# Channels-first inputs, kG transposed on TensorE and one weight row per FFN step in a gated linear attention with a gated FFN

## The chip, the cores and the metric

The kernel runs on one core of a Trainium2 chip. The metric is device time in microseconds (us). The engines are TensorE (PE; its weight loads are PEld), VectorE (DVE), ScalarE (ACT), GpSimd (POOL) and SyncE (SP), which here only issues transfers.

## The reference

For batch 4, 8 heads, 768 positions and 48 channels per head, a state of 48 x 48 per head is decayed by channel and added to, position by position; the outputs are the tokens of a gated feed-forward net (FFN).

```
state = alpha[t][:, None] * state + outer(k[t], v[t])
y[t]  = q[t] @ state
x     = y, heads side by side                   # 3072 x 384
gate  = 1 / (1 + exp(-(x @ w_gate)))            # w_gate, w_val 384 x 1536
out   = (gate * (x @ w_val)) @ w_out            # w_out 1536 x 384
```

q, k, v and alpha come as float32, the three weights as float64.

## The kernel before

**Attention.** The work is cut into 32 units, each of 384 tokens and two heads; four units (a group) fill the 384 x 384 tile of tokens that one FFN group needs, and there are eight groups. A unit treats its tokens in six chunks of 64, so that the recurrence becomes products. Its two heads lie on partitions 0 to 47 and 64 to 111, channels on partitions and tokens along the row.

- alpha, k and q are loaded with tokens on partitions (L343) and turned to `az`, `kT`, `qT` by VectorE (`turn`, L377).
- `G` (L386) is a scan of alpha backwards, the product of alpha to the end of a chunk; `F` (L398) a scan of its inverse; `dec` (L393) the decay over a chunk; `kt = kT * G` (L397); `xa`, `xb` = `qT * F`, one half per head (L411).
- The products of a unit on TensorE are the scores `kt^T x` (L425), masked to the lower triangle by VectorE (L460) or GpSimd (L455); what each chunk adds to the state (L470), for which `kn`, the turned `kt`, is the stationary operand; and the outputs (L511). `kn` comes for units 0 to 9 from TensorE transposes (L420) and four ScalarE copies (L438), and from unit 10 on (`TV`) from eight VectorE transposes (L443).
- The six states before the chunks are VectorE's (`st`, L489), their decayed copies GpSimd's or VectorE's (L502). The output is split into an exact pair of parts of twelve bits, `yt` (L529, L535), and written by transfers into the group's token tile `x` (L542).

**FFN.** A group has 12 steps; a step is 128 hidden channels of 384 tokens. `pg` and `pv` (L184) are nine products of 128 x 384 each: three tiles of input channels times three pairings of the parts. ScalarE makes `sg = sigmoid(pg)` (L580), VectorE `hf = pv * sg` (L581), ScalarE its high part `hh` (L583), GpSimd its low part `hl` (L586). The nine return products into three banks `po` (L596, with h as the stationary operand) of step n stand on TensorE behind `pg` and `pv` of step n + 1. At a group's end `po` goes through `ob` (L610) to the output.

**Weights.** A third of a step's weights (gate, value or out) is one transfer of 384 KB into one of four raw buffers (L304). Turning float64 into two parts takes per third: a scaling (ScalarE, L306), a shift (ScalarE L310 or VectorE L313), an and (VectorE L315), a shift-or (VectorE L317), the high part (ScalarE, L320) and the low part (GpSimd or VectorE, L322). All this is done once, during group 0; later groups find the weights in SBUF.

**Order.** Every part of the program is given to `Plan` with an engine, an estimated time and a key that says when it is wanted; the planner lays the parts out with these and writes each engine's instruction list. Tables by unit (`UNITS`, `SHIFTS`, `LOWS`) say which engine has a piece. The first two groups of units run as fast as they can, mixed with the weights; from group 1 on a unit is put between `pv` and `po` of every third step. 45 small products (`warm`, L563) come ahead of step 0.

## Time and profile before

| | us |
|---|---|
| device time, median of 3 runs (lowest, highest) | 625.47 (624.29, 626.53) |
| the profiled execution's span, first to last instruction | 622.7 |
| TensorE busy | 571.5 (92%) |
| VectorE busy | 444.6 (71%) |
| ScalarE busy | 214.9 (35%) |
| GpSimd busy | 264.5 (42%) |

The profiled execution's span is 2.8 us under the median of the device times: what lies before the first and behind the last instruction shown is not in the span. Busy shares over the span mix three stages: up to 45 us step 0 has not begun; up to 154 us the weights arrive and steps 0 to 11 run; from 179 us on TensorE has work all the time.

### The profile page before, as it was taken

How to read it: one execution, taken by the hardware profiler on the slowest of the kernel's cores; microseconds unless marked ns; L12 is line 12 of the kernel's file. 1: busy time of each engine (PE TensorE's matmuls, PEld its weight loads, DVE VectorE, ACT ScalarE, POOL GpSimd, SP SyncE). 2: the span in 40 equal slices, each digit the busy share in tenths (PEclk: the TensorE clock that was granted, in tenths of full speed). 3: DMA queues.
4: the chain of work that ended last, by engine and by line, in shares of the span. 5: the costliest groups of instructions: out<-in, count | busy, mean ns of one | idle time of the engine just before them, and what ended most of it. 6: DMA issues, size and time to landing. Idle time of an engine off the chain costs nothing.

```text
span 622.7 us, 13152 instructions
## 1 busy us (share of the span) xinstructions
PE 571.5 (92%) x5069; PEld 534.1 (86%) x5069; DVE 444.6 (71%) x1013; ACT 214.9 (35%) x515; POOL 264.5 (42%) x301
## 2 busy tenths in 40 slices
PE   6786867688889999999999999999999999999995
PEld 3566756567779999999899999999999999999994
DVE  8998999999987777888677777777777755211111
ACT  2558677575222222222222232222222221222121
POOL 5546597663433333434344444333344433212210
PEclk8968997999999999999999999999999999999998
DMA  9977954874345161423416161505141111001001
GB/s 193 231 201 185 235 148 139 196 225 105 103 99 132 26 155 47 114 54 88 119 31 138 31 176 28 133 20 155 41 104 30 46 51 30 20 20 39 1 0 44
DMA packets 58759, 61.20 MB, mean 98 GB/s; under 512 B 29440, under 2 KB 41728, under 8 KB 58688
## 3 DMA queue, kind: packets, MB, share of 16 engines
q1 hardware_dynamic: 58496, 59.99, 39.0%
q8 instruction: 41, 0.67, 0.5%
q0 software_dynamic: 192, 0.30, 0.2%
q14 instruction: 30, 0.25, 0.1%
HBM read 46.10 MB, written 4.72 MB: 82 GB/s over the span
## 4 chain that ended last, share of the span: by engine, by line
PE 55%; DVE 23%; DMA 10%; issue 5%; ACT 3%; SPq 3%; POOL 0%; DVEq 0%; ACTq 0%
PE pv L184 17%; PE po L596 17%; PE pg L184 16%; DVE kn L443 3%; DVE st L489 3%; DVE wraw L315 3%; DMA out_dram<-ob 2%; DVE wraw L317 2%; PE at L511 2%; PE at L425 2%; SPq L343 2%; PE at L470 2%; DMA raw_a<-in_alpha_dram 1%; DVE hf L581 1%; DVE az L377 1%
## 5 line engine op out<-in xcount | busy, mean ns | idle before, releaser
L586 POOL TENSOR_TENSOR hl<-hf,hh 128x384 fp32r<-128x384 f32 x95 | 99.6, 1048 | 239.1 <-ACT hh L583 237.6
L581 DVE TENSOR_TENSOR hf<-pv,sg 128x384 f32<-128x384 f32 x96 | 53.2, 554 | 133.9 <-PE pv L184 133.0
L184 PE MATMUL pg<-x,wgh 128*128 128x384 f32 x576 | 118.3, 340 | 10.2 <-ACT wgh L320 6.4
L184 PE MATMUL pv<-x,wvh 128*128 128x384 f32 x576 | 118.7, 341 | 8.9 <-DVE hf L581 6.3
L184 PEld LDWEIGHTS pg<-x,wgh 128*128 128x128 f32 x576 | 101.5, 189 | 12.9 <-ACT wgh L320 7.6
L184 PEld LDWEIGHTS pv<-x,wvh 128*128 128x128 f32 x576 | 101.7, 190 | 12.6 <-DVE hf L581 8.9
L583 ACT CAST hh<-hf 128x384 fp32r<-128x384 f32 x96 | 49.4, 514 | 180.5 <-DVE hf L581 180.3
L596 PE MATMUL po<-woh,hh 128*128 128x384 f32 x288 | 100.9, 350 | 2.2 <-ACT hh L583 2.2
L596 PE MATMUL po<-woh,hl 128*128 128x384 f32 x288 | 98.2, 342 | 1.2 <-POOL hl L586 1.1
L596 PE MATMUL po<-wol,hh 128*128 128x384 f32 x288 | 97.7, 339 | 0.0
L580 ACT ACTIVATE sg<-pg 128x384 f32<-128x384 f32 x96 | 46.9, 489 | 135.7 <-PE pg L184 135.6
L184 PE MATMUL pv<-x,wvl 128*128 128x384 f32 x288 | 67.0, 339 | 2.2 <-POOL wvl L322 2.0
L184 PE MATMUL pg<-x,wgl 128*128 128x384 f32 x288 | 67.1, 340 | 0.8 <-DVE wgl L322 0.7
L443 DVE STREAM_TRANSPOSE kn<-kt 32x192 f32<-32x192 f32 x176 | 65.1, 370 | 2.4
L596 PEld LDWEIGHTS po<-woh,hh 128*128 128x128 f32 x288 | 54.7, 190 | 4.7 <-ACT hh L583 2.7
L411 POOL TENSOR_TENSOR xb<-qT,F 64x384 f32<-64x384 f32 x28 | 36.7, 1312 | 49.5 <-PE at L511 47.0
L596 PEld LDWEIGHTS po<-woh,hl 128*128 128x128 f32 x288 | 54.6, 190 | 2.5 <-POOL hl L586 2.3
L184 PEld LDWEIGHTS pv<-x,wvl 128*128 128x128 f32 x288 | 51.4, 189 | 4.1 <-POOL wvl L322 2.9
L596 PEld LDWEIGHTS po<-wol,hh 128*128 128x128 f32 x288 | 54.7, 190 | 0.0
L184 PEld LDWEIGHTS pg<-x,wgl 128*128 128x128 f32 x288 | 51.8, 190 | 2.1 <-DVE wgl L322 1.0
L489 DVE SCALAR_TENSOR_TENSOR st<-st,dec,at 128x48 f32<-128x48 f32 x180 | 46.5, 258 | 4.4
L386 DVE TENSOR_TENSOR_SCAN G<-az,d1g 128x384 f32<-128x384 f32 x32 | 33.6, 1052 | 0.2
(172 smaller groups left out, 906.0 us busy)
## 6 DMA issues: line engine op xcount, KB each, us to landing
x<-yt SPq DMA_DIRECT2D x48, 144.0 KB, 3.0
wraw<-in_moe_w_val_dram SPq DMA_DIRECT2D x12, 384.0 KB, 4.5
wraw<-in_moe_w_gate_dram SPq DMA_DIRECT2D x12, 384.0 KB, 4.2
wraw<-in_moe_w_out_dram SPq DMA_DIRECT2D x12, 384.0 KB, 4.1
out_dram<-ob SPq DMA_DIRECT2D x21, 192.0 KB, 2.1
raw_a<-in_alpha_dram SPq DMA_DIRECT2D x28, 140.0 KB, 3.8
raw_k<-in_k_dram SPq DMA_DIRECT2D x28, 140.0 KB, 2.9
raw_q<-in_q_dram SPq DMA_DIRECT2D x28, 140.0 KB, 3.4
```

Source lines behind the costliest of these rows:

```text
L184: nc.tensor.matmul(out=dst, lhsT=lhs(a, i), rhs=rhs(b, i), start=(n == 0 and i == 0), stop=(n == len(todo) - 1 and i == NK - 1))
L315: plan.add("vector", 0.27, key, lambda: nc.vector.tensor_scalar(out=half[:, :, :, 0, 1], in0=half[:, :, :, 1, 1], scalar1=0x8000, scalar2= ...
L317: plan.add("vector", 0.47, key, lambda: nc.vector.scalar_tensor_tensor(out=lower, in0=upper, scalar=3, in1=lower, op0=ALU.logical_shift_le ...
L386: plan.add("vector", 0.47, t[0], lambda: nc.vector.tensor_tensor_scan(out=G[:, ::-1], data0=az[:, N:0:-1], data1=d1g, initial=0.0, op0=ALU ...
L411: plan.add(e, 0.96 if e == "gpsimd" else 0.47, t[2], lambda x=x, lo=lo, hi=hi, e=e: getattr(nc, e).tensor_tensor(out=x[lo:hi], in0=qT[lo:h ...
L443: plan.add("vector", 0.27, t[10], lambda fr=fr, to=to, par=par, late=late: nc.vector.transpose(out=kn[to:to + 32, :, 32 * late:32 * late + ...
L489: nc.vector.scalar_tensor_tensor(out=st[:, c + 1, :], in0=st[:, c, :], scalar=dec[:, c:c + 1], in1=pd[:, c * D:(c + 1) * D], op0=ALU.mult, ...
L580: plan.add("scalar", 0.38, key + 1.5, lambda: nc.scalar.activation(out=sg, in_=got["g"][1][:, 0:N], func=AF.Sigmoid), [got["g"][0]], [sgn])
L581: plan.add("vector", 0.47, key + 2.9, lambda: nc.vector.tensor_tensor(out=hf, in0=got["v"][1][:, 0:N], in1=sg, op=ALU.mult), [got["v"][0], ...
L583: plan.add("scalar", 0.41, key + 2.9, lambda: nc.scalar.copy(out=hh, in_=hf), [hfn], [hhn])
L586: plan.add(e, 0.47 if last else 0.96, key + 2.9, lambda: getattr(nc, e).tensor_tensor(out=hl, in0=hf, in1=hh, op=ALU.subtract), [hfn, hhn] ...
L596: nc.tensor.matmul(out=pt[:, 0:DM], lhsT=h[a][:, t * P:(t + 1) * P], rhs=weights.part("o", b, f), start=(f == 0 and i == 0), stop=(f == NF ...
```

## The change

The computation is the same, with the same units, steps and pairs of parts. What moves:

- **Inputs.** The host lays alpha, k and q out channels first (`laid_out`, layout only): per head pair and unit one row for each of 128 partitions with a0 (alpha at the chunks' starts), az (alpha with zeros there), k and q, 1159 numbers, 593 KB, with the unused partitions included; v likewise in chunks. The VectorE turns L377, the copy of a0 and the memsets of az are gone. k times G is written in place (L380 after), by GpSimd for every unit.
- **kG.** It is transposed on TensorE (L403 after, three products with the identity) and copied by ScalarE for every unit; the VectorE transposes L443 are gone.
- **Weights.** One transfer per step of 1.18 MB (`weights_in[f]`, L309 after), converted in two halves of 576 columns (step 0: three of 384). The shift is always ScalarE's (L322 after), the low part always GpSimd's (L330 after); VectorE has the and (L324) and the shift-or (L326). Two raw buffers in place of four of a third of the size: steps 0, 2, 4, 6, 8, 10 and 11 use the first, the others the second, whose place is later that of step 11's weights.
- **FFN step.** `hf` overwrites `sg`, of which there is one buffer. In the return, w_out is stationary and h moves, and the products with `hh` of all three banks stand ahead of those with `hl`. The output leaves transposed (the host turns it back), through three buffers that lie in the first raw buffer.
- **Engines and order.** Masks are always VectorE's, the decayed states always GpSimd's, q times F one half each (L394). All loads are issued by SP; before, GpSimd issued v of the first two units. A unit's products are spread over three steps. There are 60 `warm` products in place of 45.

```diff
-        plan.add("vector", 0.47, t[0], lambda: turn(az[:, 0:N], 0), loaded[u, 0], [an])
...
+        plan.add("sync", (0.475, P * (hi - lo) * 4 / 250e3), t["load"], lambda lo=lo, hi=hi: nc.sync.dma_start(
+            out=tin[:, lo:hi], in_=rows[b, p, :, base + lo:base + hi]), writes=[(inn, m) for m in marks])
...
+        a0, az, kT, qT = tin[:, a_0:a_z], tin[:, a_z:a_k], tin[:, a_k:a_q], tin[:, a_q:col]
...
-        turned = u >= TV
-        if not turned:
-            plan.add("tensor", (0.325, 0.9), t[9], transposes, [ktn], [pkn])
...
-                        out=kn[to:to + 32, :, 32 * late:32 * late + 32],
-                        in_=kt[fr:fr + 32].rearrange("p (c s) -> p c s", c=NC)[:, :, 32 * par:32 * par + 32]),
...
+        plan.add("tensor", (0.109 * nb, 0.9), t["X"], transposes, [(inn, "k")], [pkn])
...
+        rn, raw = raws[f % 2 if f < NF - 1 else 0]
+        plan.add("sync", (0.475, 4.9), key - 1.0, lambda: nc.sync.dma_start(out=raw.rearrange("p a b -> p (a b)"), in_=weights_in[f]),
+                 writes=[((rn, i), m) for i in range(3) for m in "ul"])
+        cuts = (0, DM, 2 * DM, WF) if f == 0 else (0, WF // 2, WF)
...
+            plan.add("gpsimd", pool_(n), kk, lambda lower=lower, lo=lo, hi=hi: nc.gpsimd.tensor_tensor(
+                out=weights.tile(f)[:, 1, lo:hi], in0=lower.bitcast(F32), in1=weights.tile(f)[:, 0, lo:hi], op=ALU.subtract),
...
-        plan.add("vector", 0.47, key + 2.9, lambda: nc.vector.tensor_tensor(
-            out=hf, in0=got["v"][1][:, 0:N], in1=sg, op=ALU.mult), [got["v"][0], sgn], [hfn])
...
+        plan.add("vector", vec(T), s - 100, lambda: nc.vector.tensor_tensor(
+            out=sg, in0=got["v"][1][:, 0:T], in1=sg, op=ALU.mult), [got["v"][0]], [sgn])
...
+                nc.tensor.matmul(out=pso_now[m][1][:, 0:T], lhsT=weights.part("o", b, f)[:, m * P:(m + 1) * P], rhs=h[a][:, 0:T],
+                                 start=(f == 0 and i == 0), stop=(f == NF - 1 and i == 2))
```

VectorE in the steady part, one unit and what stands around it (`st` is a state, `pv` times `sg` the gated product). Before:

```order
L460 TENSOR_TENSOR xa_130<-at_154,mask 64x384
L460 TENSOR_TENSOR xb_132<-at_154,mask 64x384
L443 STREAM_TRANSPOSE kn_133<-kt_127 32x6x32 x8
L377 STREAM_TRANSPOSE kT_124<-raw_k_78 128x12x32
L581 TENSOR_TENSOR hf_147<-pv_158,sg_146 128x384
L398 SCALAR_TENSOR_TENSOR F_122<-az_80,d1f_82 128x384
L377 STREAM_TRANSPOSE qT_125<-raw_q_79 128x12x32
L386 SCALAR_TENSOR_TENSOR G_121<-az_81,d1g 128x384
L377 STREAM_TRANSPOSE az_80<-raw_a_77 128x12x32
L389 TENSOR_SCALAR G_115<-G_121 128x6
L393 TENSOR_TENSOR dec_119<-a_113,G_121 128x6
```

After, the same pieces of a unit:

```order
L542 TENSOR_TENSOR sg_111<-pv_120,sg_111 128x384
L371 SCALAR_TENSOR_TENSOR G_92<-in_78,d1g 128x384
L373 TENSOR_SCALAR G_96<-G_92 128x6
L378 TENSOR_TENSOR dec_98<-in_78,G_92 128x6
L375 RECIPROCAL d1f<-G_96 128x6
L376 SCALAR_TENSOR_TENSOR F_94<-in_78,d1f 128x384
L542 TENSOR_TENSOR sg_111<-pv_120,sg_111 128x384 x2
L394 TENSOR_TENSOR xa_88<-in_78,F_94 64x384
L457 SCALAR_TENSOR_TENSOR st_109<-st_109,dec_101,at_117 128x48 x6
L506 TENSOR_TENSOR yt_86<-at_118,yt_86 128x384
L440 TENSOR_TENSOR xa_89<-at_118,mask 64x384
```

The eight transposes to `kn` and the three turns are gone; the scans read the loaded tile `in`, and the unit's other pieces stand between the same FFN products as one list.

SP while the weights come, the transfers of the weights (`wraw` before, `raw` and `first_w` after) and what stands between them (`x` is the token tile, `va` and `vb` hold v). Before:

```order
L304 DMA wraw_143<-in_moe_w_gate_dram 128x3x256
L542 DMA x_145<-yt_135 48x768 x2
L304 DMA wraw_141<-in_moe_w_out_dram 128x768
L343 DMA raw_a_77<-in_alpha_dram 32x2x560 x2
L343 DMA raw_k_78<-in_k_dram 32x2x560
L304 DMA wraw_144<-in_moe_w_val_dram 128x3x256
L343 DMA raw_k_78<-in_k_dram 32x2x560 x3
L373 DMA va_86<-in_v_dram 64x6x48
L373 DMA vb_88<-in_v_dram 64x6x48
L304 DMA wraw_142<-in_moe_w_gate_dram 128x3x256
```

After:

```order
L514 DMA x_756<-yt_86 48x768
L359 DMA in_79<-in_rows_dram 128x1159
L514 DMA x_756<-yt_86 48x768
L309 DMA raw_84<-in_w_dram 128x2304
L364 DMA va_81<-in_vc_dram 64x288
L364 DMA vb_83<-in_vc_dram 64x288
L514 DMA x_756<-yt_87 32x768
L309 DMA first_w_76<-in_w_dram 128x2304
L514 DMA x_756<-yt_87 16x768
L359 DMA in_78<-in_rows_dram 128x1159
L364 DMA va_80<-in_vc_dram 64x288
L514 DMA x_756<-yt_87 48x768
```

A row of weights for `raw` or `first_w` now waits for the conversion of the row before it in that place, and loads of units and writes of tokens stand behind it.

TensorE in the steady part, a step with a unit. Before:

```order
L596 MATMUL po_161<-woh_64,hl_153 128x384
L184 MATMUL pg_157<-x_933,wgh_1228 128x384 x6
L184 MATMUL pg_157<-x_933,wgl_1242 128x384 x3
L184 MATMUL pv_158<-x_933,wvh_1265 128x384 x6
L184 MATMUL pv_158<-x_933,wvl_1271 128x384 x3
L511 MATMUL at_156<-xa_129,va_85 48x64
L511 MATMUL at_156<-xb_131,vb_87 48x64 x2
L511 MATMUL at_156<-xa_129,va_85 48x64 x2
L511 MATMUL at_156<-xb_131,vb_87 48x64 x2
L511 MATMUL at_156<-xa_129,va_85 48x64 x2
L511 MATMUL at_156<-xb_131,vb_87 48x64 x2
```

After, a step with the transposes of one unit (the outputs, adds and scores stand in other steps):

```order
L555 MATMUL po_122<-hl_115,w_804 128x384
L555 MATMUL po_123<-hl_115,w_804 128x384
L213 MATMUL pg_119<-x_110,w_1024 128x384 x9
L403 MATMUL at_118<-ident,in_79 128x128 x3
L213 MATMUL pv_120<-x_110,w_1024 128x384 x9
L555 MATMUL po_121<-hh_112,w_949 128x384 x2
L555 MATMUL po_122<-hh_112,w_949 128x384 x2
L555 MATMUL po_123<-hh_112,w_949 128x384 x2
L555 MATMUL po_121<-hl_114,w_949 128x384
L555 MATMUL po_122<-hl_114,w_949 128x384
L555 MATMUL po_123<-hl_114,w_949 128x384
```

Before, the small products of a unit stand together between `pv` and `po`; after, the three transposes stand alone between `pg` and `pv`, and the return has its `hh` products first.

## Rows read from the trace of the kernel before

**Rows 1.** This is the busy time of each engine in four stretches. Columns: stretch, its length, then for each engine the busy us and the instructions, PEclk (the granted clock of TensorE as a share of full speed), the busy share of the DMA engines, GB/s. The edges are the starts of `pg` of step 0 (45.48), step 12 (153.79) and step 16 (178.72) and the end of the last product (615.29).

```profile
0.00:45.48 45.48, 34.59 (x471) 22.15 (x472) 41.91 (x104) 20.89 (x57) 25.24 (x45) 0.81 0.93 209
45.48:153.79 108.31, 83.18 (x713) 71.48 (x712) 105.31 (x197) 75.79 (x163) 69.44 (x63) 0.94 0.67 178
...
178.72:615.29 436.57, 433.30 (x3779) 422.15 (x3779) 273.15 (x662) 110.57 (x275) 161.04 (x183) 1.00 0.27 66
615.29:622.70 7.41, 0.01 (x1) 0.00 (x0) 0.43 (x1) 0.48 (x1) 0.00 (x0) 0.74 0.27 91
```

**Rows 2.** This is the fourth part of the page, the chain that ended last, by engine.

```profile
PE 55%; DVE 23%; DMA 10%; issue 5%; ACT 3%; SPq 3%; POOL 0%; DVEq 0%; ACTq 0%
```

**Rows 3.** This is the chain that ended last, one FFN step with a unit and the start of the next (start, us, what).

```profile
398.69 1.56 PE pv L184 x9
400.26 0.81 PE at L511 x24
401.06 0.67 PE at L470 x24
401.74 0.71 PE at L425 x24
402.45 1.77 PE po L596 x9
404.22 1.56 PE pg L184 x9
```

**Rows 4.** This is the same chain at the end: the last step's 18 return products.

```profile
612.14 3.17 PE po L596 x18
```

**Rows 5.** This is TensorE's instructions in order of time, an early unit: its three transposes of `kt`, then the scores.

```profile
14.83 0.55 PE L420 MATMUL po<-ident,kt 128*128 128x128 f32 x3
15.31 0.92 PE L425 MATMUL at<-xa,kt 48*64 48x64 f32 x24
```

**Rows 6.** This is VectorE's instructions in order of time, about one unit and two FFN steps of the steady part (start, us, line, operation, out<-in). A start-to-start distance is what one costs in the row of instructions.

```profile
402.38 1.76 DVE L489 SCALAR_TENSOR_TENSOR st<-st,dec,at 128x48 f32<-128x48 f32 x6
404.15 0.56 DVE L460 TENSOR_TENSOR xa<-at,mask 64x384 f32<-64x384 f32 x1
...
405.29 3.05 DVE L443 STREAM_TRANSPOSE kn<-kt 32x192 f32<-32x192 f32 x8
408.37 0.88 DVE L377 STREAM_TRANSPOSE kT<-raw_k 128x384 f32<-128x384 f32 x1
409.10 0.54 DVE L581 TENSOR_TENSOR hf<-pv,sg 128x384 f32<-128x384 f32 x1
409.57 0.93 DVE L398 TENSOR_TENSOR_SCAN F<-az,d1f 128x384 f32<-128x384 f32 x1
410.42 0.85 DVE L377 STREAM_TRANSPOSE qT<-raw_q 128x384 f32<-128x384 f32 x1
411.13 1.04 DVE L386 TENSOR_TENSOR_SCAN G<-az,d1g 128x384 f32<-128x384 f32 x1
412.08 0.85 DVE L377 STREAM_TRANSPOSE az<-raw_a 128x384 f32<-128x384 f32 x1
412.79 0.15 DVE L389 TENSOR_SCALAR G<-G 128x6 f32<-128x6 f32 x1
...
413.28 0.56 DVE L581 TENSOR_TENSOR hf<-pv,sg 128x384 f32<-128x384 f32 x1
```

**Rows 7.** This is the same view in the first part: two of the state updates of the first units, one after the other with others between.

```profile
35.81 0.28 DVE L489 SCALAR_TENSOR_TENSOR st<-st,dec,at 128x48 f32<-128x48 f32 x1
35.99 0.28 DVE L489 SCALAR_TENSOR_TENSOR st<-st,dec,po 128x48 f32<-128x48 f32 x1
```

**Rows 8.** This is groups of VectorE's and ScalarE's instructions in the stretch of steps 0 to 11 (count, busy us, mean ns), then the two VectorE lines by themselves with their minimum, median and maximum in ns.

```profile
L315 DVE TENSOR_SCALAR wraw<-wraw 128x384 uint16<-128x384 uint16 x32 | 25.7, 803 | 1.0 <-ACT wraw L310 0.7
L317 DVE SCALAR_TENSOR_TENSOR wraw<-wraw 128x384 uint32<-128x384 uint32 x31 | 22.3, 722 | 0.0
...
L310 ACT ACTIVATE wraw<-wraw 128x384 uint16<-128x384 uint16 x19 | 20.3, 1070 | 0.0
L306 ACT ACTIVATE wraw<-wraw 128x384 f32<-128x384 f32 x32 | 18.4, 575 | 1.5 <-DMA wraw<-in_moe_w_val_dram 1.5
...
L315 DVE TENSOR_SCALAR wraw<-wraw x32: 560/626/1430, 48.0 to 153.3; 128x384 uint16<-128x384 uint16 x32
...
L317 DVE SCALAR_TENSOR_TENSOR wraw<-wraw x31: 528/570/1359, 48.9 to 149.4; 128x384 uint32<-128x384 uint32 x31
```

**Rows 9.** This is GpSimd's instructions in order of time: one in the stretch of steps 0 to 11, one in the steady part.

```profile
86.23 3.41 POOL L322 TENSOR_TENSOR wol<-wraw,woh 128x384 fp32r<-128x384 f32 x1 [0.19 <-ACT woh L320]
...
397.99 1.01 POOL L586 TENSOR_TENSOR hl<-hf,hh 128x384 fp32r<-128x384 f32 x1 [3.12 <-ACT hh L583]
```

**Rows 10.** This is the sixth part of the page, one of its transfers (count, KB each, us from issue to landing), the stretch from 20 to 40 us, and the transfer on the chain ahead of step 0.

```profile
wraw<-in_moe_w_gate_dram SPq DMA_DIRECT2D x12, 384.0 KB, 4.2
...
20.00:40.00 20.00, 14.99 (x233) 10.27 (x229) 19.51 (x48) 11.30 (x29) 12.92 (x16) 0.71 0.99 231
...
42.48 2.65 DMA x<-yt
```

**Rows 11.** This is the fifth part of the page, ScalarE's two groups of an FFN step (count, busy us, mean ns, idle before).

```profile
L583 ACT CAST hh<-hf 128x384 fp32r<-128x384 f32 x96 | 49.4, 514 | 180.5 <-DVE hf L581 180.3
L580 ACT ACTIVATE sg<-pg 128x384 f32<-128x384 f32 x96 | 46.9, 489 | 135.7 <-PE pg L184 135.6
```

More of the change, by code (lines that the diff above doesn't have):

```diff
@@ L27, with cut, width @@
 NF = DF // P
-NT = N // P
-J = N // 32
+NM = DM // P
+WF = 3 * DM
+T = 384
+HALF = S // 2
+J = HALF // 32
 NRAW = (J - 1) * D + 32
-TURNS = [(c, (c + i) % 2) for c in range(NC) for i in range(2)]
 G_BOUND = 1e15
+def cut():
+    groups, parts, room = [], [], T
+    for b in range(B):
+        at = 0
+        while at < S:
+            n = min(room, S - at)
+            parts.append((b, at, n))
+            at, room = at + n, room - n
+            if not room:
+                groups.append(parts)
+                parts, room = [], T
+    return groups
+GROUPS = cut()
+NG = len(GROUPS)
+def width(n):
+    return n // C + 3 * n + 1
 class Plan:
@@ L119, with __init__ @@
 class Ring:
[L122 to L124 removed]
+    def __init__(self, tiles, early=()):
+        self.tiles, self.early, self.at = list(tiles), list(early), -1
     def next(self):
@@ L169, in gla_then_glu @@
     make_identity(nc, ident)
-    flags = const.tile([P, 2 * NG * NP], F32, name="flags")
+    n_units = sum(len(parts) for parts in GROUPS) * NP
+    flags = const.tile([P, 2 * n_units], F32, name="flags")
     weights = Weights(const)
@@ L487, in states @@
+        st, sn = sts[p], ("st", p)
+        if t0:
+            prev = [x[2] for parts in GROUPS for x in parts if x[0] == b and x[1] + x[2] == t0][0] // C
+            plan.add("gpsimd", 0.28, t["G"], lambda: nc.gpsimd.tensor_copy(out=st[:, 0, :], in_=st[:, prev, :]), writes=[sn])
+        else:
+            plan.add("gpsimd", 0.08, t["G"], lambda: nc.gpsimd.memset(st[:, 0, :], 0.0), writes=[sn])
         def states(lo, hi):
@@ L548, in chunked @@
-    xparts = {}
-    def xin(g):
-        if g % 2 == len(r_x):
-            r_x.append(const.tile([P, NK, 2, N], F32R, name="x1", tag="x1"))
-        return r_x[g % 2]
-    def engine(u, what, half):
-        how = UNITS[what][min(u, 8)]
-        return "gpsimd" if how == "p" or (how == "m" and half) else "vector"
+                m = min(left, P - row)
+                plan.add("sync", (0.475, m * n * 8 / 250e3), t["y"], lambda row=row, m=m, kk=kk, src=src: nc.sync.dma_start(
+                    out=xin(g)[row:row + m, kk, :, off:off + n].bitcast(F32), in_=yt[src:src + m, :, 0:n].bitcast(F32)), [(ytn, 0), (ytn, 1)],
+                    [(x_n, kk, ch, off), *(before("x1") if g == 1 else [])])
@@ new lines, in step @@
+            for tiles in ([range(NK - 1), range(NK - 1, NK)] if s < 2 else [range(NK)]):
+                plan.add("tensor", (MM * 3 * len(tiles), 1.0), s + dt, lambda nm=nm, pt=pt, tiles=tiles: products(
+                    nc, pt[:, 0:T], lambda a, i: weights.part(nm, a, f)[:, i], lambda b, i: xin(g)[:, i, b, :], tiles),
+                    [*weight(nm, f), *(x for x in xparts[g] if x[1] in tiles)], [pn])
+        (sgn, sg), (hhn, hh), (hln, hl) = r_sg.next(), r_hh.next(), r_hl.next()
+        plan.add("scalar", act(T), s - 100, lambda: nc.scalar.activation(out=sg, in_=got["g"][1][:, 0:T], func=AF.Sigmoid), [got["g"][0]], [sgn])
@@ L587, in step @@
         h = (hh, hl)
-        for t in range(NT):
-            if f == 0:
-                pso[t] = r_po.next()
-            pn, pt = pso[t]
-            def back(some, t=t, pt=pt):
-                for i in some:
-                    a, b = ((0, 0), (0, 1), (1, 0))[i]
-                    nc.tensor.matmul(out=pt[:, 0:DM], lhsT=h[a][:, t * P:(t + 1) * P], rhs=weights.part("o", b, f),
-                                     start=(f == 0 and i == 0), stop=(f == NF - 1 and i == 2))
-            for some, hs in (((0, 1), [hhn]), ((2,), [hln])) if last else (((0, 1, 2), [hhn, hln]),):
-                plan.add("tensor", (0.163 * len(some), 1.0), key_out + (t + 0.75 * some[0] if last else 0.0), lambda some=some, back=back: back(some),
-                         [*hs, ("o", f, 0), ("o", f, 1)], [pn])
@@ L791 @@
     r = _run(nc, [arrays], core_ids=[0])
-    got = tuple(r.results[0][f"out_{i}_dram"] for i in range(len(_OUTS)))
-    return got[0]
+    return _np.ascontiguousarray(r.results[0]["out_0_dram"].T)
```

686 lines of the change are left out of this document (317 added, 369 removed).

## The prediction

> **What bounds the kernel now.** I read the busy time by stretches first [rows 1], because a share over the whole span mixes stages. Three stages show. Up to 45.48 us step 0 has not begun, VectorE is busy 41.91 us and the DMA engines 93% of the time. From 45.48 to 153.79 us, while steps 0 to 11 run and the weights are converted, VectorE is busy 105.31 of 108.31 us (97%) and TensorE 83.18. From 178.72 us on TensorE is busy 433.30 of 436.57 us, VectorE 273.15. Then the chain of waits [rows 2]: PE has 55% of it, DVE 23%, DMA 10%. So the first 154 us belong to VectorE with the transfers close behind, and the last 437 to the number of products. One step costs pg 1.56, pv 1.56 and return 1.59 (18 products in 3.17), so 4.71 us [rows 3, 4]. A unit in it costs .81 + .67 + .71 and makes the return 1.77 instead of 1.59, together 2.37 [rows 3].
>
> **The first stage.** Gone from VectorE are the turns: 16 of them in the profiled start, each .71 to .73 from one start to the next (410.42 to 411.13, 408.37 to 409.10) [rows 6], with the small work on az some 12 us. What is left up to the last `yt` of unit 3: memsets 1.00 to about 4.1 us, some 3.1; four units of G .95, F .85, small ones .34, q times F .47, mask .57, `yt` .47 [rows 6] and six states of .18 [rows 7], near 4.7 each, say 19; the and and shift-or of row 0, three times about 1.2 [rows 8], 3.6; half of row 1's, .9. Sum 26.6. At 92% busy, as in the stretch before (41.91 of 45.48 [rows 1]), that is 29 us from 1.0, so 30. Then the token transfer as now, 2.65 us [rows 10], and pg of step 0 starts at about 32.5 in place of 45.48. The transfers are no bound there: four units of .74 MB with v and row 0 of 1.18 are 4.1 MB, 20 us at 209 GB/s [rows 1]. The first gated product comes at about 41, because VectorE's list has some 10 us more ahead of it (G to q times F of two units 5.4, states 1.8, the rest of row 1).
>
> **Steps 0 to 11.** Here I work out three bounds.
>
> VectorE: between the gated products of steps 0 and 11 its list holds seven units, eleven gated products and 20 half rows (and, shift-or, 576 columns). A unit is G, F, small ones, half of q times F, two masks (404.15 to 405.29, 1.14), states 1.77 and `yt`, 6.1 us [rows 6]; 7 x 6.1 + 11 x .47 = 47.9. An and with its shift-or of 384 columns takes .560 + .528 at the least, .803 + .722 in the mean, 1.43 + 1.36 at the longest [rows 8]. For 576 columns I take 1.5 times the least less .16 of fixed time, 1.47, and add the excess of the mean (.437) or of the longest (1.70): 1.9 or 3.17. Twenty of them: 29.4 at the least, 38 in the mean, 63 at the longest. Sum 77, 86 or 111; I take 86, the mean being what this kind of mixture gave. At 97% busy [rows 1] 89 us: the last gated product at 130.
>
> Weight buffers: with two, two rows per cycle, a buffer is refilled after its conversion. A transfer of 1.18 MB at 209 to 231 GB/s [rows 1, 10] lasts 5.1 to 5.6, with some 2 us until it lands (a 384 KB transfer takes 4.2 [rows 10], of which 1.7 to 1.9 are bytes) 7.2. The conversion is ScalarE's two scalings and shifts, 2 x (.76 + 1.5) by 1.5 times .575 and 1.070 less a little [rows 8], then the second half's and and shift-or 1.9, its high part (as wide as a scaling, .76) and GpSimd's low part, 1.5 times the 1.01 that GpSimd takes for 384 columns [rows 9], with little work in its way 1.6: 8.8, and .4 for the hops: 9.2. Cycle 16.4; with no stretched operation 16, with each behind one other instruction 18 to 21. Row 0's low parts end at about 38; row 2 then takes a transfer and a conversion and is ready at about 54; rows 4, 6, 8, 10 and 11 follow in the same place, so step 12 starts at 54 + 5 x 16.4 = 136. While SP waits for such a buffer, loads of units and token writes stand behind it in its queue; group 1 needs its last token tile only at step 12, so I price that at nothing, up to one cycle's rest of about 4 us for one unit if a write falls behind row 11.
>
> Transfers: ten rows (11.8 MB), seven units (5.2) and the token writes (2) are 19 MB, at 209 to 231 GB/s 82 to 91 us from about 38 us: 120 to 129.
>
> ScalarE has 20 halves of 3.0 us, 60, and its other work of that stretch (75.79 [rows 1] less the 38.7 of rows 8 and some 18 for the high parts), 19, so 79. GpSimd has 20 x 1.6 + 11 x 1.01 and for each of seven units kt, half of q times F and the states, 3.6 by their columns: 68. TensorE has 11 x 4.71 and seven units, 71. All three stay under the bounds above. Because bounds of 130, 136 and 129 take turns, I add 3% of the 97 us between, and put step 12 at 140 (before 153.79). With every VectorE operation at its least the buffers still set 134, with every one at its longest 41 + 115 = 156: the ends of this part.
>
> **The steady part.** In the profile 80 steps and 23 units remain at 178.72; after, 84 steps and 21 units remain at 140. A unit's three pieces cost .81 + .67 + .71 as now; three transposes .48 (14.83 to 15.31 [rows 5]); spread over three places, each return to full-width products costs the .18 seen once before [rows 3], three times, .54: 3.2 per unit in place of 2.37. The split itself is not in the trace: the ends are no cost at all (2.7 per unit, 11 us less in the sum) and twice the .18 (11 us more); I take the row's own .18. The eight transposes to kn cost VectorE 3.08 [rows 6] and TensorE nothing, so here the change takes .48 and more from the engine that bounds. 84 x 4.71 = 395.6, the last return 1.6, 21 x 3.2 = 67.2, less 1.2 for units that fall beside other waits; tail 7.41 [rows 1]. Sum 470.6. The same sum for before, 178.72 + 80 x 4.71 + 23 x 2.37 + 1.6 + 7.4, gives 619.0 of 622.7; the rest are gaps, which I take to lie at the boundaries of groups, where two output buffers are shared by three banks, and which I leave out with three. VectorE gets 8 of 17 us per three steps there, no bound. The chain with one `sg` buffer, sg .49, product .55, hh .51, hl 1.01 [rows 6, 9, 11] and hops, is about 3.2 us of a 4.71 us step: no wait.
>
> Span 140 + 470.6 = 610.6; the median lies 2.8 us above the profiled span, so **613 us**. Own range of this case, step 12 at 134 to 147 and a steady part some 5 us to either side: 602 to 621.
>
> **Rivals.** *VectorE and GpSimd stand in each other's way.* VectorE's ands spread from .560 to 1.430 us and one GpSimd subtraction took 3.41 us in place of 1.01 [rows 8, 9]. GpSimd would now be busy 70 of 86 us instead of 69.44 of 108.31. If GpSimd holds VectorE up and each of the 40 operations waits for half a GpSimd instruction of 1.5 us four times in five, .6 us, the halves take 29.4 + 24 and the sum is 101, at 97% 104: the last product at 145, step 12 at 149, 622 us. Against it: the mean of before has only .2 us of excess per operation [rows 8]. The Trainium skill (SBUF — State Buffer, section "Who interferes with whom") says that VectorE in a two-port mode, or with two inputs in SBUF, and GpSimd exclude each other for whole instructions, whoever comes first; the spread in rows 8 agrees with it, and by it alone the rival would hold.
>
> *Slower: the two weight buffers.* If a cycle becomes 21 us (every stage of the conversion behind another instruction of its engine; half rows cannot overlap beyond two), step 12 starts at 54 + 105 = 159 and the time is 632. It decides from 19.6 us per cycle on, where it equals before. For it speaks that in before the stretched operations reach two and three times their least [rows 8, 9] and that ScalarE and GpSimd meet the conversion behind units and FFN steps; against it that the mean ones give 16.4.
>
> *Slower: one `sg` buffer.* If the chain through ScalarE, VectorE and GpSimd, with a unit's work in front, exceeds a step by .3 us, 84 steps give 25 us: 638. It decides from .15 us on. Against: 1.5 us of slack.
>
> *The kG trade only.* If the first two stages gave nothing, the transposes alone would cost 21 x .83: 643; the removed turns make that unlikely, and it is counted with the slower ones.
>
> **How the numbers follow.** Forecast .60; the GpSimd rival .15; weight buffers .10; the rest of the slower side .04; better than 602 us (the weight stage at its least, or transposes hidden) .07; between 623.6 and 627.3, by the boundary gaps and the dearer splits together, .04. The measurement can tell .3% from no change, so 623.6 and 627.3 are the borders. Faster: .60 + .07 + .11 of the first rival = .78; the same: .03 of it and .04 = .07; slower .10 + .04 and the last .01 of that rival = .15. The range 598 to 629 leaves out the slow end and the best few.
>
> **What would show it.** In the profile after: the first pg near 32 us; VectorE near 97% busy between steps 0 and 11; the mean of the half-row and and shift-or near .95 each (rival one: 1.3 and more); SP's waits for a raw buffer and products waiting for a weight's low part (rival two); step 12 near 140; then 4.71 per step, and in a unit's three places 3.2 together. TensorE below 98% busy past step 12, waiting for `hl` or `sg`, would prove rival three, and step 0 later than 38 us or step 12 later than 152 would prove the forecast wrong.

## The result, and the profile after

The changed kernel takes 630.76 us (median of 4 runs, 628.65 to 632.23), the kernel before in the same runs 624.92: a ratio of 1.0083, 95% interval 1.0056 to 1.0109. It is slower by 0.8%. The forecast was 613 us, with a range of 598 to 629, and so most likely a faster kernel.

The busy time by stretches of the changed kernel's profile, columns as in [rows 1]; the edges are the starts of `pg` of step 0 and step 12 and the end of the work on `po`.

```profile
0.00:30.20 30.20, 27.07 (x446) 17.10 (x447) 27.17 (x73) 17.37 (x46) 13.92 (x28) 1.00 0.69 223
30.20:159.70 129.50, 96.85 (x882) 81.39 (x881) 109.28 (x178) 88.41 (x170) 90.66 (x75) 0.92 0.47 152
159.70:621.10 461.40, 460.68 (x3826) 444.80 (x3824) 181.19 (x394) 136.49 (x359) 153.87 (x178) 1.00 0.20 56
```

Read against [rows 1], the difference lies in one stretch. Step 0 begins at 30.20 us, 15.3 earlier than before. Steps 0 to 11 then take 129.50 us, 21.2 longer. From step 12 to the end it is 468.8 us against 468.9: TensorE is busy 460.68 of 461.40 us. So 15.3 us were won, 21.2 lost, and the spans differ by 5.8 (628.5 against 622.7).

In the long stretch no engine is full: VectorE is busy 84% of it (97% before), the transfers 47% (67% before). Something other than the amount of work holds it. SyncE's instructions in order of time show what; these are the transfers of weight rows into the first raw buffer (start, duration of the issue):

```profile
34.24 0.54 SPq L309 DMA_DIRECT2D raw<-in_w_dram  x1
...
101.22 0.33 SPq L309 DMA_DIRECT2D raw<-in_w_dram  x1
...
144.48 0.33 SPq L309 DMA_DIRECT2D raw<-in_w_dram  x1
```

These are rows 2, 8 and 11; rows 4, 6 and 10 (issued at 58.38, 79.14 and 122.06) are left out. A turn is the time from one transfer into a buffer to the next one into it. From 34.24 to 144.48 are five turns, 22.0 us each in the mean (20.8 to 24.1). Row 11 is the last; its conversion ends at 158.7 and step 12 starts at 159.7. One turn, that of row 6 (issued at 79.14, landed at 84.2), in order of time on ScalarE:

```profile
89.20 0.52 ACT L383 ACTIVATE junk<-F 128x384 bf16<-128x384 f32 x1 [2.42 <-DVE F L376]
89.63 0.19 ACT L383 ACTIVATION_READ_ACCUMULATOR junk<-F 128x1 f32 x1
89.72 0.72 ACT L321 ACTIVATE raw<-raw 128x576 f32<-128x576 f32 x1
...
98.51 0.71 ACT L328 CAST w<-raw 128x576 fp32r<-128x576 f32 x1 [2.77 <-DVE raw L326]
```

on VectorE:

```profile
93.95 1.76 DVE L457 SCALAR_TENSOR_TENSOR st<-st,dec,at 128x48 f32<-128x48 f32 x6
95.63 1.75 DVE L324 TENSOR_SCALAR raw<-raw 128x576 uint16<-128x576 uint16 x1
```

and on GpSimd:

```profile
96.64 1.16 POOL L465 TENSOR_TENSOR va<-st,dec 48x288 f32<-48x288 f32 x1
97.88 1.07 POOL L465 TENSOR_TENSOR vb<-st,dec 48x288 f32<-48x288 f32 x1
99.02 0.77 POOL L451 COPY st<-st 128x48 f32<-128x48 f32 x1
99.75 1.45 POOL L330 TENSOR_TENSOR w<-raw,w 128x576 fp32r<-128x576 f32 x1
```

The row lies ready from 84.2, but ahead of its first scaling ScalarE's list has a sum for the check of alpha (L383), which waits 2.42 us for `F`; the scaling starts at 89.72. Later VectorE has the six states of a unit ahead of the second half's `and`, ScalarE waits 2.77 us for the second shift-or, and GpSimd has a unit's decayed states (L465) and a copy between the two low parts. At 101.2 the buffer is free and the next row is issued at once. Over the five rows that free the buffer for another (2, 4, 6, 8, 10) the means are: 6.5 us from issue to landing, 4.3 until the first scaling, 11.2 from there to the end of the last low part; sum 22.0. In the 11.2 us eight instructions follow one another (the scalings and shifts of both halves, then the `and`, the shift-or, the high part and the low part of the second half). They take 8.76 us in the mean; 2.45 us lie between them.

While row 11 is converted, ScalarE, VectorE and GpSimd have nothing else to do. ScalarE's first and GpSimd's last instruction of it:

```profile
149.65 0.71 ACT L321 ACTIVATE raw<-raw 128x576 f32<-128x576 f32 x1 [1.92 <-DMA raw<-in_w_dram]
...
157.23 1.44 POOL L330 TENSOR_TENSOR w<-raw,w 128x576 fp32r<-128x576 f32 x1 [1.49 <-ACT w L328]
```

It lands after 5.1 us, is begun at once, and is converted in 9.0 us: 14.2 us from issue to end, with 8.78 us of instructions and .23 between them.

Loads of units and token writes that stand behind a weight row in SP's list do not hold the stretch: between 30 and 160 us no instruction of VectorE or GpSimd waits for a transfer, ScalarE waits once (1.9 us, for row 11) and TensorE once (1.5 us, for a token write).

VectorE's groups in the same stretch (from 30 to 160 us), those that answer to the unit of [rows 6]:

```profile
L371 DVE TENSOR_TENSOR_SCAN G<-in,d1g 128x384 f32<-128x384 f32 x9 | 11.9, 1321 | 0.0
L376 DVE TENSOR_TENSOR_SCAN F<-in,d1f 128x384 f32<-128x384 f32 x9 | 11.8, 1316 | 0.3
L373 DVE TENSOR_SCALAR G<-G 128x6 f32<-128x6 f32 x9 | 8.9, 985 | 0.0
L542 DVE TENSOR_TENSOR sg<-pv,sg 128x384 f32<-128x384 f32 x12 | 6.6, 550 | 4.5 <-PE pv L213 4.2 <-ACT sg L541 0.2
```

The scans take 1.32 us (F .93 and G 1.04 in [rows 6]), the maximum of 128x6 numbers .985 (.15 there); the product that reads PSUM keeps its .55.

The steady part, the chain that ended last, three steps with one unit (as [rows 3]):

```profile
398.82 1.57 PE pg L213 x9
400.38 0.84 PE at L418 x24
401.23 1.76 PE pv L213 x9
...
406.14 0.33 PE at L403 x3
406.47 1.58 PE pv L213 x9
...
412.76 0.81 PE at L499 x24
413.57 0.67 PE at L425 x24
414.24 1.78 PE po L555 x9
```

From 398.82 to 416.02 are 17.20 us: three steps of 4.71 and a unit of 3.07 (the steps' other products, left out here, stand at 1.56 to 1.58 as in [rows 3, 4]). The unit is made of scores .84 with .20 for the slower `pv` behind them, transposes .33 with .02, outputs and adds .81 + .67 with .19. Before it was 2.37.

### The profile page after: what moved, and what is told of

Its sections match the earlier page's. It is cut to its first block, busy times and chain, and to the rows that moved or that the text cites. A ratio compares the mean times of both kernels' runs of the same rounds, so it can differ in the third digit from the quotient of the medians.

```text
span 628.5 us, 12861 instructions
## 1 busy us (share of the span) xinstructions
PE 584.6 (93%) x5150; PEld 543.3 (86%) x5150; DVE 317.6 (51%) x645; ACT 242.3 (39%) x573; POOL 258.5 (41%) x281
## 4 chain that ended last, share of the span: by engine, by line
PE 76%; DVE 13%; ACT 3%; issue 3%; POOL 2%; DMA 1%; DVEq 0%; ACTq 0%; POOLq 0%
PE po L555 22%; PE pv L213 22%; PE pg L213 22%; PE at L499 3%; PE at L418 3%; PE at L425 2%; DVE F L376 2%; DVE G L371 2%; ACT raw L322 1%; DVE st L457 1%; DVE G L373 1%; DVE raw L326 1%; PE at L403 1%; DVE raw L324 1%; DVE first_w L324 1%
## 5 line engine op out<-in xcount | busy, mean ns | idle before, releaser
L547 POOL TENSOR_TENSOR hl<-sg,hh 128x384 fp32r<-128x384 f32 x95 | 102.8, 1082 | 231.9 <-ACT hh L544 230.2
L213 PE MATMUL pg<-x,w 128*128 128x384 f32 x864 | 173.4, 344 | 7.7 <-ACT w L328 5.9
L213 PE MATMUL pv<-x,w 128*128 128x384 f32 x864 | 172.2, 342 | 0.8 <-POOL w L330 0.7
L213 PEld LDWEIGHTS pg<-x,w 128*128 128x128 f32 x864 | 155.6, 193 | 10.0 <-ACT w L328 6.3
L542 DVE TENSOR_TENSOR sg<-pv,sg 128x384 f32<-128x384 f32 x96 | 53.3, 555 | 203.9 <-PE pv L213 203.4
L213 PEld LDWEIGHTS pv<-x,w 128*128 128x128 f32 x864 | 150.1, 189 | 3.2 <-POOL w L330 1.0
L555 PE MATMUL po<-hh,w 128*128 128x384 f32 x576 | 122.4, 347 | 9.6 <-ACT hh L544 9.5
L555 PEld LDWEIGHTS po<-hh,w 128*128 128x128 f32 x576 | 101.3, 190 | 12.8 <-ACT hh L544 11.4
L555 PE MATMUL po<-hl,w 128*128 128x384 f32 x288 | 66.6, 339 | 5.7 <-POOL hl L547 5.7
L394 POOL TENSOR_TENSOR xb<-in,F 64x384 f32<-64x384 f32 x28 | 33.8, 1207 | 63.2 <-PE at L499 58.6
L555 PEld LDWEIGHTS po<-hl,w 128*128 128x128 f32 x288 | 52.0, 188 | 7.2 <-POOL hl L547 7.1
L371 DVE TENSOR_TENSOR_SCAN G<-in,d1g 128x384 f32<-128x384 f32 x30 | 32.0, 1066 | 23.1 <-DMA in<-in_rows_dram 19.7
L380 POOL TENSOR_TENSOR in<-in,G 128x384 f32<-128x384 f32 x30 | 28.7, 957 | 22.6 <-DVE G L371 17.2
L330 POOL TENSOR_TENSOR w<-raw,w 128x576 fp32r<-128x576 f32 (+1 forms) x15 | 23.1, 1552 | 14.1 <-ACT w L328 9.3
```

The costliest lines, as they stand in the source:

```text
L213: nc.tensor.matmul(out=dst, lhsT=lhs(a, i), rhs=rhs(b, i), start=(n == 0 and i == 0), stop=(n == len(todo) - 1 and i == NK - 1))
L371: plan.add("vector", 0.09 + 2 * n / 900, t["G"], lambda: nc.vector.tensor_tensor_scan(out=G[:, ::-1], data0=az[:, n:0:-1], data1=d1g[:, 0: ...
L394: plan.add(e, vec(n) if e == "vector" else pool_(n), t["q"], lambda x=x, lo=lo, hi=hi, e=e: getattr(nc, e).tensor_tensor(out=x[lo:hi], in0 ...
L542: plan.add("vector", vec(T), s - 100, lambda: nc.vector.tensor_tensor(out=sg, in0=got["v"][1][:, 0:T], in1=sg, op=ALU.mult), [got["v"][0]] ...
L547: plan.add(e, vec(T) if last else pool_(T), s - 100, lambda: getattr(nc, e).tensor_tensor(out=hl, in0=sg, in1=hh, op=ALU.subtract), [sgn, ...
L555: nc.tensor.matmul(out=pso_now[m][1][:, 0:T], lhsT=weights.part("o", b, f)[:, m * P:(m + 1) * P], rhs=h[a][:, 0:T], start=(f == 0 and i == ...
```

## The experiments

Theory A: two raw buffers set the end of steps 0 to 11. Theory B: VectorE and GpSimd hold each other up there, and the buffers only follow. Each run's ratio is to the kernel before (624.5 to 625.0 us in these runs).

| run | us | ratio, 95% interval |
|---|---|---|
| e1, third raw buffer | 616.15 | 0.9852 [0.9828, 0.9876] |
| e2, half-row transfers | 616.71 | 0.9877 [0.9847, 0.9907] |
| e3, low parts on VectorE | 627.52 | 1.0038 [1.0024, 1.0052] |
| e4, three banks per unit | 625.38 | 1.0008 [0.9998, 1.0017] |
| e9, conversion ahead of units | 634.78 | 1.0148 [1.0119, 1.0177] |
| e6, e1 and e4 | 609.65 | 0.9759 [0.9740, 0.9777] |
| e7, e6 and kn by VectorE | 599.77 | 0.9597 [0.9581, 0.9613] |
| e8, e7 and e2 | 600.36 | 0.9611 [0.9595, 0.9627] |
| e11, e7 and e9 | 604.99 | 0.9678 [0.9661, 0.9695] |
| e13, e7 with a fourth raw buffer | 596.14 | 0.9543 [0.9527, 0.9559] |

**e1, a third raw buffer.**

```diff
+    raws.append(("raw2", sb.tile([P, WF, 2], U32, name="raw2")))
...
-        rn, raw = raws[f % 2 if f < NF - 1 else 0]
+        rn, raw = raws[(0, 1, 2, 0, 1, 2, 0, 1, 2, 0, 2, 0)[f]]
```

> A third raw buffer for the weight rows, all else as in the changed kernel. Theory A (two buffers bound steps 0 to 11: the first one turns every 22.1 us and five turns lead to step 12 at 159.7 us): rows 3, 6, 9 and 11 follow row 0 in that place, four turns instead of five with step 12 at 142 us or earlier, and since VectorE's 109 us of work then binds, between 138 and 148; time 609 to 619 us. Theory B (VectorE and GpSimd hold each other up, the buffers only follow): VectorE's work is as long as before, step 12 within 4 us of 159.7, time 627 to 634 us.

616.15 us, as theory A had it. The stretch of steps 0 to 11 in its profile:

```profile
30.50:141.70 111.20, 90.36 (x754) 77.24 (x753) 96.69 (x152) 82.77 (x149) 83.53 (x65) 0.89 0.51 168
```

Step 12 starts at 141.7. The instructions are still stretched (from 30 to 160 us G takes 1.33, F 1.14 and the shift-or 1.03 us in the mean), so the stretching alone does not make 159.7. Fewer pieces of units are done when step 12 begins: nine units have their outputs, eleven in the changed kernel. By the costs of the steady part above, the scores of one unit, adds and outputs of two and transposes of three, which come later here, are 5.4 us. That is why 18 us in this stretch are 13 in the span (615.6 against 628.5).

**e2, two transfers per row.**

```diff
-        plan.add("sync", (0.475, 4.9), key - 1.0, lambda: nc.sync.dma_start(out=raw.rearrange("p a b -> p (a b)"), in_=weights_in[f]),
-                 writes=[((rn, i), m) for i in range(3) for m in "ul"])
+        for part in range(1 if f == 0 else 2):
...
+                     writes=[((rn, i), m) for i in (range(3) if f in (0, 2) else [part]) for m in "ul"])
```

> Still two raw buffers, but each row comes as two transfers of half a row, and each half waits only for the conversion of its own half. Theory A: the first half's transfer (about 4 us) runs beside the conversion of the second half (about 4 us), a turn falls from 22.1 to about 18, step 12 at 137 to 145 us, time 608 to 616 us. Theory B: step 12 within 4 us of 159.7, time 627 to 634 us.

616.71 us, just above theory A's range and far from theory B's. A turn of the first half's place takes 18.5 us (33.91 to 126.54 for five), and step 12 starts at 145.5 us, 14.2 earlier than in the changed kernel and half a us behind theory A's range. With the same two buffers and the same bytes, freeing them by halves gives nearly what a third buffer gives.

**e3, the low parts on VectorE.**

```diff
-            plan.add("gpsimd", pool_(n), kk, lambda lower=lower, lo=lo, hi=hi: nc.gpsimd.tensor_tensor(
+            e = "vector" if f >= 1 else "gpsimd"
+            plan.add(e, vec(n) if e == "vector" else pool_(n), kk, lambda lower=lower, lo=lo, hi=hi, e=e: getattr(nc, e).tensor_tensor(
```

> The low parts of the weights of steps 1 to 11 are made by VectorE instead of GpSimd: GpSimd loses 37.5 us of work between steps 0 and 12, VectorE gains 22 instructions of some 0.75 us. Theory A (buffers): a turn gets shorter only by the faster last instruction (1.7 us to 0.75) and less waiting for GpSimd, to about 20 us, step 12 near 150, time 619 to 624 us. Theory B (VectorE and GpSimd hold each other up): the scans F and G, now 1.32 us in the mean there, return to 0.9 to 1.0, VectorE's stretched work falls by 25 us or more, and step 12 comes at 145 or earlier, time below 616 us.

627.52 us: neither. The stretch from 30.2 to 160 us, and VectorE's groups in it:

```profile
30.20:160.00 129.80, 100.23 (x899) 84.16 (x898) 112.30 (x201) 90.32 (x172) 57.70 (x55) 0.91 0.47 154
```

```profile
L377 DVE TENSOR_TENSOR_SCAN F<-in,d1f 128x384 f32<-128x384 f32 x9 | 9.7, 1080 | 0.2
L372 DVE TENSOR_TENSOR_SCAN G<-in,d1g 128x384 f32<-128x384 f32 x9 | 9.2, 1022 | 0.0
```

GpSimd falls from 90.66 to 57.70 us and the scans from 1.32 to 1.02 and 1.08: the stretching goes with GpSimd's work. But VectorE has the low parts' 19.45 us on top, is 3 us busier than in the changed kernel, and the turn of the first buffer stays at 21.6 us (34.4 to 142.6 for five). The eight instructions of a row take 7.95 us in place of 8.76, but the waits ahead of them and between them add up to 7.1 us in place of 6.8. So taking the last instruction from GpSimd does not shorten the turn; how much of that is VectorE's new work the run does not separate.

**e9, the conversion ahead of the units.**

```diff
-        weight_piece(f, -50 + 0.0 if f == 0 else -20.0 if f == 1 else f - 2.0)
+        weight_piece(f, -50 + 0.0 if f == 0 else -20.0 if f == 1 else f - 14.0)
```

> Two raw buffers as in the changed kernel, but the planner's keys put the conversion of a weight row ahead of units and copies of kn (12 steps earlier), so that ScalarE, VectorE and GpSimd meet it sooner; the amount of work is the same. If the 22.1 us turn holds much waiting in the engines' lists (3.6 us ahead of the first scaling, and some of the 11.2 us of conversion), a turn falls to 17 to 19 us, step 12 starts 10 to 20 us earlier in spite of the two buffers, with fewer units done by then (some 2.2 us later each), time 612 to 622 us. If the turn is the work itself (instructions stretched by sharing between VectorE and GpSimd, transfers), it stays above 20.5 us and the time within 626 to 633 us.

634.78 us, slower than either branch; the turn, 22.4 us (31.2 to 143.4), is as the second branch had it. But the work itself did not grow. Over rows 2, 4, 6, 8 and 10 a row's instructions take 8.74 us (8.76 in the changed kernel), the wait ahead of the first scaling is 3.4 us (4.3), and 4.2 us lie between the instructions (2.45): the waiting moved into the conversion. The loss comes with the last row. Its transfer leaves 1 us earlier than in the changed kernel (143.4), but it then waits 6.4 us for ScalarE (nothing there), whose list has a unit's copies of `kn` ahead of it. This order of the lists did not replace a buffer; no other order was tried.

**e4, three banks per unit.**

```diff
         else:
-            pdn, pd = bank.next()
+            pdn, pd = pkn, pk
```

> The sums for the state go into the bank of the transposed kG (as in the kernel before), so a unit needs three banks instead of four. Theory A for the steady part (what a unit costs more than before is the transposes, 0.33 us, and the scores standing alone between pg and pv, 0.33 us, because their bank is free only after yt): the scores stand beside outputs and adds again, three steps with a unit take 16.87 us instead of 17.20, 21 units give 7 us, time 622 to 626 us. Theory B (the transposes alone make the difference to before, and their place does not matter): three steps stay at 17.20, time 629 to 632 us.

625.38 us. The chain that ended last, a unit's outputs, adds and scores in the steady part:

```profile
410.96 0.81 PE at L499 x24
411.77 0.67 PE at L425 x24
412.44 0.71 PE at L418 x24
```

The three stand together again; twelve steps take 67.48 us (68.79 in the changed kernel), so 16.87 per three, as theory A had it. By the code, with four banks per unit and three in the ring, the bank of the scores is that of the outputs of the unit before, so the scores had to wait until that unit had left it. From step 12 to the end are 459.3 us (468.8 in the changed kernel), but step 12 comes 4.9 us later, at 164.6, so that some 5 us are left of the gain.

**e6, e1 and e4 together.** Both edits above.

> Third raw buffer and three banks per unit together. If the two gains are independent (616.15 for the first alone, 5.4 us for the second alone): 610 to 612 us, three steps with a unit at 16.87 us. If the scores' place costs in steps 0 to 11 what it gains later (the second alone moved step 12 from 159.7 to 164.6 us): 613 to 617 us.

609.65 us, .35 below the first branch: the gains add up.

**e7, kn by VectorE as well.** From unit 10 on the eight transposes of the kernel before (its L443) stand in place of the TensorE transposes and ScalarE copies:

```diff
+        turned = u >= 10
+        if not turned:
+            pkn, pk = bank.next()
...
+                if turned:
...
+                        plan.add("vector", 0.39, t["kn"], lambda fr=fr, to=to, par=par, late=late: nc.vector.transpose(
```

> As the run with third raw buffer and three banks, and from unit 10 on the turned kG comes from eight transposes on VectorE, as in the kernel before, not from TensorE and ScalarE. If kG on TensorE is paid in full where TensorE binds (0.33 us per unit): 16.50 to 16.55 us per three steps, 21 or 22 units, 6 to 8 us less than that run, 602 to 606 us. If VectorE's 3.08 us per unit come in the way of the gated products: no gain, 609 us or more.

599.77 us, 9.9 below e6, more than the 6 to 8 expected. Twelve steps take 65.84 us, 16.46 per three: .41 less than in e6, the transposes' .33, the .02 behind them, and what else changed place with them; times 21 units that is 8.6. So the TensorE transposes of kG are paid in full in the steady part.

**e11, e7 with e9's keys; e8, e7 with half-row transfers; e13, e7 with `raws[f % 4]` and two more raw buffers.**

> All of it: third raw buffer, three banks, kn by VectorE from unit 10 on, and the conversion ahead of the units. If waiting in lists still lengthens the rows' turns with three buffers: step 12 at 130 to 138 us and the time 2 to 8 us below the same kernel with the old keys. If VectorE's sum binds with three buffers: units are only moved behind step 12, time within 3 us of that kernel.

604.99 us, 5.2 slower than e7: neither branch. The rows are converted by 126.4 us, 15 earlier than in e7, and step 11 starts at 123.8 (138.3 in e7). But step 12 starts only at 147.5 (140.8): between the two TensorE's list now has the outputs of three units and other pieces of theirs (none in e7), which wait for VectorE and GpSimd, and VectorE is nearly full:

```profile
123.78:147.52 23.74, 17.27 (x239) 15.19 (x235) 22.30 (x51) 8.17 (x28) 15.43 (x19) 0.80 0.45 132
```

The units were only moved, as in the second branch, and this cost 5 us in place of at most 3.

> Third raw buffer with half-row transfers, three banks, kn by VectorE from unit 10 on. If transfers and buffers no longer bind with three buffers: within 3 us of 599.77. If the shorter first transfer of a row still lets the conversion begin earlier: 592 to 597 us.

600.36 us, no gain over e7: with three buffers, freeing them by halves gives nothing.

> A fourth raw buffer beside the third, with three banks per unit and kn by VectorE from unit 10 on (599.77 us with three buffers). If with three buffers the engines that convert bind, and the rows already wait for ScalarE (7.0 us in the mean after landing): no gain, 597 to 602 us. If a buffer still binds: row 11 is ready 5 us earlier or more and the time is 596 us or less.

596.14 us, 3.6 us below e7. This lies between the branches, .14 above the second. Its rows are converted by 135.2 us, 6.3 earlier than in e7 (141.5), as the second branch had it: with three buffers a buffer still bound. Step 12 starts at 134.7 us, and from 140 us on TensorE has no gap:

```profile
30.20:140.00 109.80, 87.87 (x788) 73.69 (x786) 102.29 (x153) 83.19 (x149) 83.68 (x66) 0.97 0.52 173
140.00:587.00 447.00, 447.00 (x3854) 437.60 (x3854) 270.86 (x595) 116.00 (x293) 160.56 (x188) 1.00 0.20 59
```

VectorE is busy 102.29 of 109.80 us (93%) up to 140 us: there it is nearly full again, as in [rows 1]. This is the fastest version, 4.6% below the kernel before.

**e12, VectorE beside GpSimd by itself.** Eight rounds of six VectorE instructions alone, then twelve beside 48 subtractions of 128x576 on GpSimd.

> A kernel by itself that computes nothing of the reference: 8 rounds of six VectorE instructions alone (the scans G and F, the maximum of 128x6, the and and the shift-or of 576 columns, the product of a PSUM bank with SBUF), then 12 rounds of the same beside a row of GpSimd subtractions of 128x576. If the stretching in steps 0 to 11 is VectorE and GpSimd holding each other up: beside GpSimd the scans take 1.3 us and more instead of 0.95, the shift-or 1.0 and more instead of 0.75, the 128x6 maximum up to 1 us instead of 0.15, GpSimd's subtraction 1.6 us and more instead of 1.44; the product out of PSUM stays at 0.55. If it comes from transfers or ScalarE: every duration is the same in both parts within 5%.

VectorE's groups in the first 34 us, alone:

```profile
L38 DVE TENSOR_TENSOR_SCAN G<-az,d1g 128x384 f32<-128x384 f32 x8 | 7.6, 947 | 0.0
L39 DVE TENSOR_TENSOR_SCAN F<-az,d1f 128x384 f32<-128x384 f32 x8 | 7.5, 935 | 0.0
L41 DVE TENSOR_SCALAR raw<-raw 128x576 uint16<-128x576 uint16 x8 | 6.4, 803 | 0.0
L42 DVE SCALAR_TENSOR_TENSOR raw<-raw 128x576 uint32<-128x576 uint32 x8 | 6.0, 751 | 0.0
L44 DVE TENSOR_TENSOR sg<-pv,sg 128x384 f32<-128x384 f32 x8 | 4.7, 589 | 0.0
L40 DVE TENSOR_SCALAR G<-G 128x6 f32<-128x6 f32 x8 | 1.2, 150 | 0.0
```

and in order of time beside GpSimd, with two of GpSimd's subtractions:

```profile
48.52 2.15 DVE L38 TENSOR_TENSOR_SCAN G<-az,d1g 128x384 f32<-128x384 f32 x1
50.59 2.08 DVE L39 TENSOR_TENSOR_SCAN F<-az,d1f 128x384 f32<-128x384 f32 x1
51.93 1.92 POOL L50 TENSOR_TENSOR d<-a,b 128x576 f32<-128x576 f32 x1
52.59 1.29 DVE L40 TENSOR_SCALAR G<-G 128x6 f32<-128x6 f32 x1
53.80 0.79 DVE L41 TENSOR_SCALAR raw<-raw 128x576 uint16<-128x576 uint16 x1
53.94 1.76 POOL L50 TENSOR_TENSOR d<-a,b 128x576 f32<-128x576 f32 x1
54.39 0.58 DVE L44 TENSOR_TENSOR sg<-pv,sg 128x384 f32<-128x384 f32 x1
54.90 1.42 DVE L42 SCALAR_TENSOR_TENSOR raw<-raw 128x576 uint32<-128x576 uint32 x1
```

The scans more than double, the shift-or goes from .75 to 1.42, the maximum of 128x6 from .15 to 1.29; the product out of PSUM stays at .59 and the `and` at .80. GpSimd's subtraction takes 1.85 us in the mean (1.44 for row 11 above). So theory B's mechanism exists, on every instruction it was expected on. Of the `and` nothing had been expected, and e12 does not settle it: the rounds run in step with GpSimd (a round takes 7.72 us, four subtractions), and the `and` always begins .14 us ahead of a subtraction, never in the middle of one. The last section comes back to this.

## Why the prediction was wrong

**The step that failed is the weight buffers' cycle.** The forecast took 16.4 us per turn and step 12 at 136, then 140. The turn measured 22.0 and step 12 came at 159.7. Of its terms the transfer was set too high (7.2, measured 6.5) and the conversion too low (9.2, measured 11.2), and the wait of a landed row for ScalarE, 4.3 us, was not in it at all. The instructions were priced right: the eight of a row take 8.76 us, stretched ones included, and the forecast had 8.8. What was left out is the waiting, 4.3 us ahead of the first instruction and 2.45 between them, for which .4 was set. The error lies in the form of the sum: it added up the instructions of a row as if each engine were free when the row came, while each of the three engines takes its list in order, and the list held steps and units between the row's pieces. Row 11, which met none of these, took 14.2 us, less than the forecast turn. The 19.7 us between 140 and 159.7 come out of this: row 2 ready at 58.4 instead of 54 (4.4; its transfer left at 34.2, some 4 earlier than forecast, but its turn took 24.1), from there to row 11's end 100.3 instead of 82 (18.3), step 12 1.0 after that, less the 4 that had been added on top.

That the buffers set the end of this stretch is shown by e1 and e2 from two sides: another buffer, or the same two freed sooner, each gives some 14 us. That a turn is so long by waiting is read from the rows of the profile. No run took the waiting out: e9 changed the order of the lists and only moved it. Which entries of the lists it hangs on stays open.

**The slower rival described what happened.** It had a cycle of 21 us, step 12 at 159 and 632 us; measured 22.0, 159.7 and 630.8. It was given a chance of .10. What spoke for it, that ScalarE and GpSimd meet the conversion behind units and FFN steps, is what the rows show; the stretched operations, its other reason, cost a row no more than was priced. That "the mean ones give 16.4" is no argument against it, since means of durations hold no waiting in lists. That its 159 came so close is partly luck: row 2 was 4.4 us later than its 54, the next four turns took 86.1 us in place of 84, and the last, row 11, 14.2 in place of 21.

**Sharing between VectorE and GpSimd was there, on other instructions.** The `and` with its shift-or was priced at 1.9 us per half row and measured 1.93 (1.009 and .925 in the mean). What had been priced at the rows of the steady part, where GpSimd is idle more than half of the time, grew: against .94 and .95 alone in e12 and .15 and .55 in the steady part of the kernel before, nine times F .38, G .37, the maximum .83 and half of q times F .36 are 17.5 us. VectorE's 109.28 us up to step 12 are 13 more than the 96 forecast (10 to the first gated product and 86), less than this sum. The rival that set .6 us on each `and` and shift-or had the mechanism, but there it came to .2. GpSimd's own work came to 90.66 us against 68, ScalarE's to 88.41 against 79 and TensorE's to 96.85 against 71, all still below the 129.5 us of the stretch. How much of the waiting comes from stretched instructions of units ahead in the lists is not settled: e3 took a third of GpSimd's work away and e9 changed the order, and the turn stayed between 21.6 and 22.4 in both.

**Two sums are slightly off.** The pieces named for a unit's VectorE work add up to 5.99 us, not 6.1, and the upper end of the case's own range, 621, leaves out the 5 us of the steady part that its lower end has; with them it is 625. Neither decides.

**The first stage held.** Step 0 starts at 30.2 us (forecast 32.5, before 45.48). VectorE is busy 27.17 of these 30.2 us (forecast 26.6 us of work). With the turns gone the stage is a third shorter, as the forecast had it and for its reason.

**The steady part held.** From step 12 the forecast had 470.6 us, measured 468.8. A unit costs 3.07 instead of the 3.2 assumed: the split costs .20, .02 and .19 behind the three pieces and .13 on the scores, the transposes .33 instead of .48. That the split comes to the .54 forecast as three times .18 is partly luck, since the places differ so much. The groups' boundaries cost nothing: each of the third to sixth groups takes 68.79 us, four times 17.20. The kG trade was seen in the right place: kG on TensorE takes the place of VectorE work that cost nothing there. e4 and e7 give back .33 and .41 us per three steps.

**The `sg` rival did not occur:** TensorE is busy 460.68 of 461.40 us from step 12 on.

## What to carry to other kernels

For a buffer that is filled and worked off by several in-order engines, add up the whole turn: transfer, the wait until the first engine's list comes to it, and the pieces with what stands between them; set the number of buffers by that, and keep a multiple of the bare sum (1.3 times here, 22.0 against 16.4) in the range where buffers get fewer. A chance for such a rival should be read from the margin: 16.4 against a break-even of 19.6 is a small one where three engines with other work in their lists take part, since here the waits alone came to 6.8 us per turn. Work that moves from an idle engine to the one that bounds is paid in full, piece by piece, and also by what it breaks apart.
